# Two on-chip reshapings of an attention, mixer and Fourier kernel moved from TensorE matmuls to small transfers

## The chip, the cores and the metric

The kernel runs on one core of a Trainium2 chip. The metric is the device time of one execution in microseconds; the time before is the median of three executions.

## The reference, cut to what matters

Three blocks follow one another: attention (2 batches, 12 heads, 448 rows, 64 wide), a token and channel mixer, and a block that adds the real part of a two-dimensional Fourier transform, normalises each row and runs a two-layer network of width 3,072.

```python
def _moe2_ref(x, w_ch1, w_ch2):
    X = np.fft.fft(x, axis=1)
    X = np.fft.fft(X, axis=2)
    u = x + np.real(X).astype(np.float32)
    mu = np.mean(u, axis=-1, keepdims=True)
    var = np.mean((u - mu) ** 2, axis=-1, keepdims=True)
    un = (u - mu) / np.sqrt(var + 1e-06)
    ch = np.maximum(un @ w_ch1, 0.0) @ w_ch2
    return (u + ch).astype(np.float32)
```

The change lies in this last block. `x` is 2 x 448 x 768.

## The kernel before

Activations are kept transposed: 768 channels as six tiles of 128 partitions (`resid[ct][b]`), 448 rows of one batch along the free side. Each float32 matmul of the networks is done as three matmuls on split operands (high by high, high by low, low by high), so a 128 x 448 group of the second network costs 18 matmuls going up (`up_chunk`, lines 233 to 235) and 24 going down (`down_tile`, lines 254 to 259). The weights arrive as 64-bit words, are loaded by SyncE's queue into two staging buffers (`fetch`, line 132) and are turned into high and low parts by six steps on ScalarE and VectorE (`convert_steps`).

The middle of the kernel, some 274 to 430 us, is written as one list of words, `ORDER2`. A word names a function and its arguments; each engine, SyncE's queue among them, works off its instructions in the order of the list. The words that matter here:

- `ro b` (`rows_fold`) folds the 448 values of channel 0 of batch b to 225 values in one partition, `r0s[b]`.
- `mr b` (`mean_rows`) turns that row into two columns, of 112 and 113 partitions, by two matmuls with a 1 x 2 block of ones, into a PSUM bank. `rh b` (`rows_high`) casts them on ScalarE, `rl b` (`rows_low`) subtracts on VectorE, and `mx b` (`mixed_mean`) uses them as stationary operands some 17 us later.
- `zh`, `zl`, `oc`, `hi`, `lo` round, split and copy the planes of the Fourier transform and the result; `lo 0.ct` makes `act_l[ct][0]`, which the first groups of the second network (`up2.0`, `up1.0`, ...) need channel tile by channel tile.
- `vm b`, `vr b`, `vi b` give the variance, its root and the inverse deviations `inv[b]`, 112 partitions x 4.
- `dv b` (`deviation`) spreads these over a 128 x 448 PSUM tile by four matmuls against the identity, with each column of `inv[b]` repeated 128 times; `dc b` (`deviation_copy`) copies the tile to `rstd[b]` on ScalarE.
- `dt c.b` (`second_down`) is a group of 24 matmuls, `dm c.b` (`scale`) multiplies its result by `rstd[b]` on VectorE.
- `ld k` loads a weight tile and `cv k.j` is step j of its conversion; `two` closes the buffers of the Fourier stage.

`bank()` hands out the eight PSUM banks in turn. `begin_fft` closes the pools whose buffers the Fourier stage reuses and opens the pool `fft1`.

Of the kernel before, what the change touches and what calls it, by code (L numbers as in the profile page):

```python
# [10 lines left out]
F32 = mybir.dt.float32  # L11
# [8 lines left out]
B, H, S, D = 2, 12, 448, 64  # L20
DM = H * D
TS = 112
NI = S // TS
# [17 lines left out]


ORDER2 = """
ld0 ld1 cv0.0 cv0.1 cv0.2 cv1.0 dn0.3 ad0.3 cv1.1 cv1.2 dn0.4 cv0.3 cv1.3 dn0.0 ad0.0 fs0.0 ad0.4 ro0 dn0.1 fd0.0
dn0.2 fo0.0 ad0.1 ad0.2 fm0.0 fz0 fv0.0 fs0.1 dn0.5 fe0.0 fd0.1 fo0.1 fv0.1 ad0.5 fs0.2 fe0.1 fh0.1 fh0.0 fl0.1 dn1.0
ad1.0 ro1 cv0.4 cv0.5 fl0.0 dn1.3 ad1.3 fm0.1 fs1.0 dn1.4 fd1.0 ld2 ld3 fe0.2 cv1.4 cv1.5 ad1.4 cv2.0 cv2.1 fm0.2 me0
mc0 fm1.0 cv3.0 cv3.1 fz1 fe1.0 fv1.0 fo1.0 dn1.1 fd0.2 ce0.5 ad1.1 fv0.2 cv2.2 fo0.2 ce0.0 dn1.2 ad1.2 fh0.2 dn1.5
ad1.5 fl0.2 fh1.0 fl1.0 fs1.1 fd1.1 fs1.2 fft ch0.0.0 ch0.3.0 ch0.2.0 ch0.2.1 ch0.0.1 ch0.1.0 ch0.1.1 fe1.1 ch0.1.2
zh0.1 fd1.2 fm1.1 fo1.1 fv1.1 ce0.2 zl0.1 ch0.0.2 zh0.0 fh1.1 fl1.1 ce0.4 zl0.0 ch0.2.2 zh0.2 zl0.2 ch0.3.1 ch0.3.2
zh0.3 zl0.3 fm1.2 mr1 mr0 fe1.2 rh1 ch1.2.0 ch1.0.0 ch1.0.1 fo1.2 fv1.2 fh1.2 cv2.3 fl1.2 sq0.0 oc0.0 sq0.1 rh0 oc0.1  # L50
cv2.4 ha0.0 cv3.2 rl1 hs0.0 fa0.0 ch1.0.2 zh1.0 rl0 ch1.3.0 ch1.2.1 ch1.2.2 zh1.2 ce0.1 zl1.0 ha0.1 zl1.2 ch1.1.0
ch1.3.1 ch1.3.2 ch1.1.1 hi0.0 zh1.3 hs0.1 ce0.3 zl1.3 fa0.1 ny0 ch1.1.2 zh1.1 zl1.1 cv2.5 nc0 ba0.0 sq0.2 oc0.2 hi0.1
me1 mc1 sq1.0 oc1.0 ha0.2 ce1.5 hs0.2 fa0.2 sq1.1 oc1.1 ba0.1 lo0.0 lo0.1 ba0.2 hi0.3 hi0.2 ha1.0 ce1.0 hi0.5 lo0.5
lo0.3 lo0.2 hi0.4 lo0.4 ce1.1 hs1.0 cv3.3 fa1.0 ce1.3 ce1.2 ce1.4 ny1 hi1.0 nc1 sq1.2 ba1.0 oc1.2 ha1.1 hs1.1 ha1.2
hs1.2 fa1.1 ba1.1 mx0 fa1.2 ba1.2 mx1 two up2.0 up1.0 cv3.4 cv3.5 up0.0 lo1.0 hi1.4 hi1.3 gh2.0 hi1.1 vs0.1 hi1.2
hi1.5 vs0.0 gh1.0 ma1 ma0 va0.1 vs0.2 va0.2 vs0.3 up3.0 gl1.0 ld4 cv4.0 ld5 cv5.0 cv4.1 cv4.2 cv4.3 ld6 va0.3 cv5.1
cv5.2 vs0.4 va0.4 cv5.3 cv4.4 cv4.5 cv5.4 gh0.0 cv5.5 lo1.3 lo1.1 lo1.2 lo1.4 lo1.5 up3.1 up1.1 up0.1 gl0.0 vs0.5
gl2.0 cv6.0 up2.1 up4.1 up4.0 vs1.0 va0.5 vs1.1 va1.1 gh0.1 gh1.1 cv6.1 cv6.2 gh3.0 gh3.1 vs1.2 va1.2 ld7 cv6.3 cv7.0
cv7.1 vs1.3 va1.3 cv6.4 cv6.5 cv7.2 cv7.3 gl3.0 gh4.1 vs1.4 gh2.1 va1.4 gl3.1 ld8 gh4.0 cv8.0 cv8.1 gl1.1 cv8.2 cv7.4
cv8.3 cv7.5 cv8.4 cv8.5 gl0.1 ld9 cv9.0 cv9.1 cv9.2 cv9.3 up5.0 gh5.0 ld10 cv10.0 up6.1 gh6.1 up7.0 gh7.0 cv10.1 gl5.0  # L60
cv10.2 cv10.3 cv9.4 cv9.5 gl2.1 vs1.5 va1.5 ld11 cv11.0 cv11.1 gl4.1 cv11.2 cv11.3 up6.0 gh6.0 cv10.4 up5.1 vm0 gh5.1
cv10.5 cv11.4 ld12 cv12.0 vr0 up7.1 gh7.1 gl6.0 gl7.0 gl4.0 cv12.1 cv12.2 cv12.3 cv11.5 gl6.1 ld13 cv13.0 gl5.1 cv13.1
cv13.2 cv13.3 vi0 cv12.4 cv12.5 cv13.4 cv13.5 ld14 ld15 vm1 gl7.1 cv14.0 cv14.1 cv14.2 cv14.3 cv15.0 dt0.0 dt0.1
cv15.1 cv15.2 cv15.3 cv14.4 cv15.4 cv14.5 cv15.5 vr1 vi1 ld16 dv0 dc0 cv16.0 ld17 cv17.0 cv16.1 cv16.2 cv16.3 ld18
cv17.1 cv17.2 cv17.3 ld19 dt1.0 dt1.1 dv1 dc1 cv16.4 cv16.5 cv18.0 cv17.4 cv18.1 cv18.2 cv17.5 cv19.0 dm0.0 dt2.1
dm0.1 cv19.1 cv18.3 cv19.2 cv19.3 dt2.0 cv18.4 cv19.4 dt4.0 dp0.5 dp0.0 da0.0 dp1.3 dp1.0 da0.1 dm1.0 dp0.3 da1.0
dm1.1 da1.1 dm2.1 dp1.1 dm2.0 cv18.5 cv19.5 dt4.1 dt3.0 dp0.4 dp0.1 da2.0 dm3.0 da3.0 dt3.1 dt5.0 da2.1 dm3.1 dp1.4
dp0.2 dp1.2 dm4.0 da3.1 dm4.1 da4.0 dm5.0 dp1.5 da5.0 dt5.1 da4.1 dm5.1 da5.1
"""
ENGINES = {getattr(mybir.EngineType, e) for e in ("PE", "DVE", "Activation", "Pool", "SP")}  # L70

# [31 lines left out]
def fused_kernel(ctx: ExitStack, tc: tile.TileContext, qk, v, w1, w2, wa, wb, wc, wd, fa, fb, out):  # L103
    nc = tc.nc
    mm = nc.tensor.matmul
    vec, act, pool = nc.vector, nc.scalar, nc.gpsimd
# [161 lines left out]
    with ExitStack() as actx:  # L268
# [6 lines left out]
            out=mask[:, S - TS :], in_=mask[:, S - TS :], pattern=[[-1, TS]], compare_op=ALU.is_ge, fill=MASKED,  # L275
# [313 lines left out]
    pb, uv, ab, r0s = {}, {}, {}, {}  # L589
# [59 lines left out]
    f1 = [None]  # L649
# [44 lines left out]
    rows_of = {}  # L694

    def mean_rows(b):
        rp = bank()
        pb["r", b] = [(TS + i, rp[: TS + i, 2 * i : 2 * i + 2]) for i in range(2)]
        for i, (rows, part) in enumerate(pb["r", b]):
            mm(part, lhsT=r0s[b][:, i * TS : i * TS + rows], rhs=ones[:, :2], start=True, stop=True)  # L700

    def rows_high(b):
        rows_of[b] = [
# [98 lines left out]
    inv, rstd, g2, pools = {}, [], {}, {}  # L802
# [64 lines left out]

    def mean_back(b, ct):
        pool.tensor_tensor(out=resid[ct][b], in0=resid[ct][b], in1=mu[b], op=ALU.add)
# [2 lines left out]
        dn=down, ad=down_add, ro=rows_fold, fs=fold_sum, fd=fold_difference, fe=fold_ends, fv=fold_even,  # L872
        fo=fold_odd, fh=fold_high, fl=fold_low, fm=fold_mean, fz=fold_zero, fft=begin_fft, ch=channel, zh=z_high, zl=z_low,
        me=mean, mc=mean_copy, ce=center, mr=mean_rows, rh=rows_high, rl=rows_low, mx=mixed_mean, ma=mixed_add,
        sq=sequence, ny=nyquist, nc=nyquist_copy, fa=forward_add, oc=odd_copy, ha=half_add, hs=half_subtract, ba=backward_add, hi=high,
        lo=low, ld=load_second, cv=convert_second, two=begin_second, up=lambda m, b: second_up(m, b, 0),
        gh=lambda m, b: second_up(m, b, 1), gl=lambda m, b: second_up(m, b, 2), vs=square, va=square_add, vm=variance,
        vr=root, vi=inverse, dt=second_down, dm=scale, da=scaled, dv=deviation, dc=deviation_copy, dp=mean_back,
    )
    with tc.manual_schedule(engines=ENGINES):  # L880
        for word in ORDER2.split():
            name = word.rstrip("0123456789.")
# [98 lines left out]
```

## Time and profile before

| what | value |
|---|---|
| time before, median of 3 (range) | 674.91 us (674.77 to 675.99) |
| the profiled execution | 674.54 us |
| span of its profile | 672.8 us |
| TensorE busy | 668.2 us, 99% of the span, 3,702 matmul records |
| VectorE busy | 533.9 us, 79% |
| ScalarE busy | 282.7 us, 42% |
| GpSimd busy | 111.3 us, 17% |
| TensorE's granted clock, mean | 0.999 of full speed |
| DMA | 73.35 MB, mean 109 GB/s |

The span runs from the first to the last instruction of the profiled execution; 1.74 us of its own time lie outside the span. One float32 matmul of the program can appear as two records. Matmuls overlap in the records, so what one costs is read from the distance between starts, not from its duration.

### The profile page before, as it was taken

How to read it: one execution, taken by the hardware profiler on the slowest of the kernel's cores; microseconds unless marked ns; L12 is line 12 of the kernel's file. 1: busy time of each engine (PE TensorE's matmuls, PEld its weight loads, DVE VectorE, ACT ScalarE, POOL GpSimd, SP SyncE). 2: the span in 40 equal slices, each digit the busy share in tenths (PEclk: the TensorE clock that was granted, in tenths of full speed). 3: DMA queues.
4: the chain of work that ended last, by engine and by line, in shares of the span. 5: the costliest groups of instructions: out<-in, count | busy, mean ns of one | idle time of the engine just before them, and what ended most of it. 6: DMA issues, size and time to landing. Idle time of an engine off the chain costs nothing.

```text
span 672.8 us, 9833 instructions
## 1 busy us (share of the span) xinstructions
PE 668.2 (99%) x3702; PEld 607.1 (90%) x3702; DVE 533.9 (79%) x1016; ACT 282.7 (42%) x601; POOL 111.3 (17%) x86
## 2 busy tenths in 40 slices
PE   9999999999999999999999999999999999999997
PEld 6777778999999999999999999999999999999997
DVE  7988876678988955899899859989878898656851
ACT  7989785433343333235465432224432334332200
POOL 0042343310000000400510007271002320000000
PEclk9999999999999999999999999999999999999999
DMA  8532221194344331200224332423332543222311
GB/s 222 189 137 70 102 75 64 39 280 142 116 166 141 126 109 48 95 0 1 95 95 145 105 127 94 141 94 120 114 123 72 181 140 123 84 92 77 118 41 55
DMA packets 20863, 73.35 MB, mean 109 GB/s; under 512 B 2366, under 2 KB 7230, under 8 KB 20448
## 3 DMA queue, kind: packets, MB, share of 16 engines
q1 hardware_dynamic: 20240, 69.48, 30.5%
q0 software_dynamic: 576, 3.25, 1.7%
q8 instruction: 29, 0.48, 0.3%
q14 instruction: 18, 0.15, 0.1%
HBM read 69.96 MB, written 2.75 MB: 108 GB/s over the span
## 4 chain that ended last, share of the span: by engine, by line
PE 99%; DMA 0%; DVE 0%; SPq 0%; issue 0%
PE psum L234 13%; PE psum L258 13%; PE psum L233 13%; PE psum L254 13%; PE psum L259 13%; PE psum L235 13%; PE psum L314 4%; PE psum L367 4%; PE psum L349 4%; PE psum L436 3%; PE psum L470 2%; PE psum L672 2%; PE psum L741 1%; PE psum L387 1%; PE psum L456 1%; DMA k<-in_qk 0%
## 5 line engine op out<-in xcount | busy, mean ns | idle before, releaser
L254 PE MATMUL psum<-gh,wh 128*128 128x448 f32 x432 | 157.2, 364 | 0.0
L233 PE MATMUL psum<-acth,wh 128*128 128x448 f32 x432 | 156.9, 363 | 0.0
L234 PE MATMUL psum<-acth,wl 128*128 128x448 f32 x432 | 156.4, 362 | 0.0
L258 PE MATMUL psum<-gh,wl 128*128 128x448 f32 x432 | 156.4, 362 | 0.0
L259 PE MATMUL psum<-gl,wh 128*128 128x448 f32 x432 | 156.0, 361 | 0.0
L235 PE MATMUL psum<-actl,wh 128*128 128x448 f32 x432 | 155.9, 361 | 0.0
L141 ACT ACTIVATE m<-w 128x512 f32<-128x512 f32 (+2 forms) x92 | 70.9, 771 | 125.4 <-DVE wl L161 83.4
L159 ACT CAST wh<-m 128x512 fp32r<-128x512 f32 (+1 forms) x90 | 63.3, 704 | 95.2 <-PE psum L259 53.6
L254 PEld LDWEIGHTS psum<-gh,wh 128*128 128x128 f32 x432 | 81.1, 188 | 5.8 <-issue 0.2
L233 PEld LDWEIGHTS psum<-acth,wh 128*128 128x128 f32 x432 | 81.1, 188 | 5.7
L235 PEld LDWEIGHTS psum<-actl,wh 128*128 128x128 f32 x432 | 80.9, 187 | 5.8
L259 PEld LDWEIGHTS psum<-gl,wh 128*128 128x128 f32 x432 | 80.9, 187 | 5.8
L258 PEld LDWEIGHTS psum<-gh,wl 128*128 128x128 f32 x432 | 81.0, 187 | 5.0 <-issue 0.2
L234 PEld LDWEIGHTS psum<-acth,wl 128*128 128x128 f32 x432 | 81.0, 188 | 4.6
L148 DVE SCALAR_TENSOR_TENSOR m<-w,m 128x512 uint32<-128x512 uint32 (+2 forms) x92 | 80.2, 872 | 2.3
L161 DVE TENSOR_TENSOR wl<-m,wh 128x512 fp32r<-128x512 f32 (+1 forms) x84 | 69.4, 829 | 14.7 <-ACT wh L159 14.3
L152 DVE SCALAR_TENSOR_TENSOR m<-w,m 128x512 uint32<-128x512 uint32 (+2 forms) x92 | 79.2, 861 | 2.0
L143 DVE TENSOR_SCALAR m<-m 128x512 f32<-128x512 f32 (+2 forms) x92 | 50.8, 552 | 34.4 <-ACT m L141 34.2
L241 DVE SCALAR_TENSOR_TENSOR gl<-psum,gh 128x448 fp32r<-128x448 f32 x72 | 43.6, 618 | 27.2 <-ACT gh L239 27.2
L239 ACT ACTIVATE gh<-psum 128x448 fp32r<-128x448 f32 x72 | 37.8, 540 | 63.1 <-PE psum L235 62.7
L337 ACT ACTIVATE p<-p,small 112x224 f32<-112x224 f32 (+3 forms) x96 | 49.6, 520 | 3.9 <-DVE small L327 3.8
L144 DVE TENSOR_SCALAR m<-m 128x512 uint32<-128x512 uint32 (+2 forms) x92 | 48.9, 532 | 2.4
(146 smaller groups left out, 741.1 us busy)
## 6 DMA issues: line engine op xcount, KB each, us to landing
w<-in_wc SPq DMA_DIRECT2D x24, 768.0 KB, 4.2
w<-in_wd SPq DMA_DIRECT2D x36, 512.0 KB, 3.2
w<-in_wa SPq DMA_DIRECT2D x12, 768.0 KB, 4.3
w<-in_wb SPq DMA_DIRECT2D x18, 512.0 KB, 3.2
v<-in_v SPq DMA_DIRECT2D x12, 224.0 KB, 2.8
out<-t SPq DMA_DIRECT2D x12, 224.0 KB, 1.9
q<-in_qk SPq DMA_DIRECT2D x11, 224.0 KB, 3.4
k<-in_qk SPq DMA_DIRECT2D x11, 224.0 KB, 3.5
```

Of the source, the lines that this page charges most:

```text
L141: act.activation(out=m, in_=hi.bitcast(F32), func=AF.Abs)
L143: vec.tensor_scalar(out=m, in0=m, scalar1=F64_MIN, scalar2=F64_MAX, op0=ALU.max, op1=ALU.min)
L148: vec.scalar_tensor_tensor(out=mu, in0=lo, scalar=29, in1=mu, op0=ALU.logical_shift_right, op1=ALU.bitwise_or)
L152: vec.scalar_tensor_tensor(out=mu, in0=hi, scalar=0xC0000000, in1=mu, op0=ALU.bitwise_and, op1=ALU.bitwise_or)
L159: act.copy(wh, m)
L161: low_engine[0].tensor_tensor(out=wl, in0=m, in1=f(wh), op=ALU.subtract)
L233: mm(pb[:, :S], lhsT=lh, rhs=act_h[ct][b], start=ct == 0, stop=False)
L234: mm(pb[:, :S], lhsT=ll, rhs=act_h[ct][b], start=False, stop=False)
L235: tail[0] = mm(pb[:, :S], lhsT=lh, rhs=act_l[ct][b], start=False, stop=ct == NCT - 1).ins
L254: mm(pb[:, :S], lhsT=lh, rhs=gh, start=j + k == 0 and seeded is None, stop=False, skip_group_check=seeded is not None,)
L258: mm(pb[:, :S], lhsT=ll, rhs=gh, start=False, stop=False, skip_group_check=seeded is not None)
L259: tail[0] = mm(pb[:, :S], lhsT=lh, rhs=gl, start=False, stop=j == last and k == nk - 1, skip_group_check=seeded is not None,).ins
```

## The change

`mean_rows` no longer runs matmuls. It takes a small SBUF tile from the pool `fft1` and fills its two columns by two transfers on SyncE's queue, from 112 and from 113 values of the one-partition row. `rows_high` and `rows_low` read the SBUF tile, each column repeated twice, instead of PSUM.

`deviation` writes `inv[b]` into a row of 448 floats in HBM, one value for each partition and column, and `deviation_copy` reads that row back into all 128 partitions of `rstd[b]`; both are transfers on SyncE's queue. The words move in `ORDER2`: `dv0 dc0` from behind `ld16` to behind `ld15` and ahead of `vm1`; `dv1 dc1` from behind `dt1.1` to behind `ld17`. The place of `mr1 mr0` is unchanged. The rest of `ORDER2` keeps its order (the diff also wraps its lines anew).

```diff
-cv13.2 cv13.3 vi0 cv12.4 cv12.5 cv13.4 cv13.5 ld14 ld15 vm1 gl7.1 cv14.0 cv14.1 cv14.2 cv14.3 cv15.0 dt0.0 dt0.1
-cv15.1 cv15.2 cv15.3 cv14.4 cv15.4 cv14.5 cv15.5 vr1 vi1 ld16 dv0 dc0 cv16.0 ld17 cv17.0 cv16.1 cv16.2 cv16.3 ld18
-cv17.1 cv17.2 cv17.3 ld19 dt1.0 dt1.1 dv1 dc1 cv16.4 cv16.5 cv18.0 cv17.4 cv18.1 cv18.2 cv17.5 cv19.0 dm0.0 dt2.1
...
+ld13 cv13.0 gl5.1 cv13.1 cv13.2 cv13.3 vi0 cv12.4 cv12.5 cv13.4 cv13.5 ld14 ld15 dv0 dc0 vm1 gl7.1 cv14.0 cv14.1
+cv14.2 cv14.3 cv15.0 dt0.0 dt0.1 cv15.1 cv15.2 cv15.3 cv14.4 cv15.4 cv14.5 cv15.5 vr1 vi1 ld16 cv16.0 ld17 dv1
+dc1 cv17.0 cv16.1 cv16.2 cv16.3 ld18 cv17.1 cv17.2 cv17.3 ld19 dt1.0 dt1.1 cv16.4 cv16.5 cv18.0 cv17.4 cv18.1
...
+    scratch = ctx.enter_context(tc.tile_pool(name="scratch", bufs=1, space=bass.MemoryType.DRAM))
...
     def mean_rows(b):
-        rp = bank()
-        pb["r", b] = [(TS + i, rp[: TS + i, 2 * i : 2 * i + 2]) for i in range(2)]
-        for i, (rows, part) in enumerate(pb["r", b]):
-            mm(part, lhsT=r0s[b][:, i * TS : i * TS + rows], rhs=ones[:, :2], start=True, stop=True)
+        rp = f1[0].tile([113, 16], F32, name=f"rows{b}")
+        pb["r", b] = [(TS + i, rp[: TS + i, i : i + 1].to_broadcast([TS + i, 2])) for i in range(2)]
+        for i in range(2):
+            nc.sync.dma_start(out=rp[: TS + i, i : i + 1], in_=r0s[b][:, i * TS : (i + 1) * TS + i])
...
     def deviation(b):
-        pb["w", b] = bank()[:, :S]
-        for i in range(NI):
-            mm(
-                pb["w", b][:, i * TS : (i + 1) * TS], lhsT=inv[b][:, i : i + 1].to_broadcast([TS, 128]),
-                rhs=ident[:TS, :TS], start=True, stop=True,
-            )
+        pb["w", b] = scratch.tile([1, S], F32, name=f"dev{b}")
+        nc.sync.dma_start(out=pb["w", b][0].rearrange("(i p) -> p i", p=TS), in_=inv[b])
 
     def deviation_copy(b):
-        act.copy(rstd[b], pb["w", b])
+        nc.sync.dma_start(out=rstd[b], in_=pb["w", b].to_broadcast([128, S]))
```

## Rows read from the trace of the kernel before

**Rows 1.** The page, part 4: the chain that ended last, by engine.

```profile
PE 99%; DMA 0%; DVE 0%; SPq 0%; issue 0%
```

**Rows 2.** Timeline, TensorE, 300.9 to 302.6: start us, us, line, what, count.

```profile
300.78 0.33 PE L672 MATMUL psum<-fal,acth 128*111 128x384 f32 x1
300.95 0.33 PE L672 MATMUL psum<-fah,actl 128*111 128x384 f32 x1
301.21 0.94 PE L700 MATMUL psum<-ones,r 1*112 1x2 f32 x8
302.09 0.43 PE L672 MATMUL psum<-fah,acth 128*113 128x386 f32 x1
302.36 0.34 PE L672 MATMUL psum<-fal,acth 128*113 128x386 f32 x1
```

**Rows 3.** Timeline, TensorE, around the two groups of deviation().

```profile
388.52 0.37 PE L259 MATMUL psum<-gl,wh 128*128 128x448 f32 x1
388.73 1.04 PE L860 MATMUL psum<-ident,r 112*128 112x112 f32 x8
...
389.83 0.36 PE L258 MATMUL psum<-gh,wl 128*128 128x448 f32 x1
...
399.03 0.37 PE L259 MATMUL psum<-gl,wh 128*128 128x448 f32 x1
...
400.33 0.36 PE L258 MATMUL psum<-gh,wl 128*128 128x448 f32 x1
```

**Rows 4.** Waits of TensorE, whole span: us in total, times, longest.

```profile
PE psum L195 <- PEq L968: 0.8, 1, 0.8
```

**Rows 5.** Timeline, VectorE, four places (in brackets: idle before, releaser).

```profile
308.15 0.22 DVE L713 TENSOR_TENSOR repl<-psum,reph 112x2 fp32r<-112x2 f32 x2
...
312.53 0.56 DVE L680 TENSOR_TENSOR zl<-psum,zh 112x384 fp32r<-112x384 f32 x1 [0.56 <-ACT zh L676]
...
320.44 0.62 DVE L784 TENSOR_TENSOR actl<-resid,acth 128x448 fp32r<-128x448 f32 x1
...
329.23 0.94 DVE L161 TENSOR_TENSOR wl<-m,wh 128x768 fp32r<-128x768 f32 x1
```

**Rows 6.** Timeline, TensorE, two places of the first `up` groups.

```profile
321.51 0.36 PE L235 MATMUL psum<-actl,wh 128*128 128x448 f32 x1
...
330.70 0.36 PE L233 MATMUL psum<-acth,wh 128*128 128x448 f32 x1
330.91 0.36 PE L234 MATMUL psum<-acth,wl 128*128 128x448 f32 x1
```

**Rows 7.** Timeline, ScalarE, 301 to 307: the casts of rows_high.

```profile
301.80 0.22 ACT L708 CAST reph<-psum 112x2 fp32r<-112x2 f32 x2
...
305.55 0.23 ACT L708 CAST reph<-psum 112x2 fp32r<-112x2 f32 x2
```

**Rows 8.** Source line 601, the folded row: ns min/median/max, first and last start.

```profile
L601 DVE TENSOR_TENSOR r<-resid x2: 371/372/373, 274.9 to 283.2; 1x223 f32<-1x223 f32 x2
```

**Rows 9.** Timeline, SyncE's DMA issues, three places.

```profile
248.76 23.87 SPq L132 DMA_DIRECT2D w<-in_wc  x4
...
382.07 0.33 SPq L132 DMA_DIRECT2D w<-in_wd  x1
...
393.84 0.33 SPq L132 DMA_DIRECT2D w<-in_wd  x1
```

**Rows 10.** Source line 841, last step of the inverse deviations.

```profile
L841 DVE TENSOR_TENSOR r<-r,nt x2: 161/162/164, 382.8 to 391.4; 112x4 f32<-112x4 f32 x2
```

**Rows 11.** Source line 851, the first reader of rstd in scale().

```profile
L851 DVE TENSOR_TENSOR t<-psum,rstd x12: 606/616/625, 405.0 to 455.3; 128x448 f32<-128x448 f32 x12
```

**Rows 12.** DMA issues of the span: count, KB each, median us to landing.

```profile
out<-t SPq DMA_DIRECT2D x12, 224.0 KB, 1.9
...
k<-in_qk SPq DMA_DIRECT2D x11, 224.0 KB, 3.5
```

**Rows 13.** DMA queue, 0 to 4 us: packets, MB, share of 16 engines.

```profile
q1 hardware_dynamic: 593, 0.49, 52.4%
```

More of the change, by code (lines that the diff above doesn't have):

```diff
@@ L43 @@
 ORDER2 = """
[L44 to L62, printed above, removed]
-cv13.2 cv13.3 vi0 cv12.4 cv12.5 cv13.4 cv13.5 ld14 ld15 vm1 gl7.1 cv14.0 cv14.1 cv14.2 cv14.3 cv15.0 dt0.0 dt0.1
@@ L64 @@
-cv15.1 cv15.2 cv15.3 cv14.4 cv15.4 cv14.5 cv15.5 vr1 vi1 ld16 dv0 dc0 cv16.0 ld17 cv17.0 cv16.1 cv16.2 cv16.3 ld18
-cv17.1 cv17.2 cv17.3 ld19 dt1.0 dt1.1 dv1 dc1 cv16.4 cv16.5 cv18.0 cv17.4 cv18.1 cv18.2 cv17.5 cv19.0 dm0.0 dt2.1
-dm0.1 cv19.1 cv18.3 cv19.2 cv19.3 dt2.0 cv18.4 cv19.4 dt4.0 dp0.5 dp0.0 da0.0 dp1.3 dp1.0 da0.1 dm1.0 dp0.3 da1.0
-dm1.1 da1.1 dm2.1 dp1.1 dm2.0 cv18.5 cv19.5 dt4.1 dt3.0 dp0.4 dp0.1 da2.0 dm3.0 da3.0 dt3.1 dt5.0 da2.1 dm3.1 dp1.4
-dp0.2 dp1.2 dm4.0 da3.1 dm4.1 da4.0 dm5.0 dp1.5 da5.0 dt5.1 da4.1 dm5.1 da5.1
+ld0 ld1 cv0.0 cv0.1 cv0.2 cv1.0 dn0.3 ad0.3 cv1.1 cv1.2 dn0.4 cv0.3 cv1.3 dn0.0 ad0.0 fs0.0 ad0.4 ro0 dn0.1
@@ new lines @@
+fd0.0 dn0.2 fo0.0 ad0.1 ad0.2 fm0.0 fz0 fv0.0 fs0.1 dn0.5 fe0.0 fd0.1 fo0.1 fv0.1 ad0.5 fs0.2 fe0.1 fh0.1 fh0.0
+fl0.1 dn1.0 ad1.0 ro1 cv0.4 cv0.5 fl0.0 dn1.3 ad1.3 fm0.1 fs1.0 dn1.4 fd1.0 ld2 ld3 fe0.2 cv1.4 cv1.5 ad1.4
+cv2.0 cv2.1 fm0.2 me0 mc0 fm1.0 cv3.0 cv3.1 fz1 fe1.0 fv1.0 fo1.0 dn1.1 fd0.2 ce0.5 ad1.1 fv0.2 cv2.2 fo0.2
+ce0.0 dn1.2 ad1.2 fh0.2 dn1.5 ad1.5 fl0.2 fh1.0 fl1.0 fs1.1 fd1.1 fs1.2 fft ch0.0.0 ch0.3.0 ch0.2.0 ch0.2.1
+ch0.0.1 ch0.1.0 ch0.1.1 fe1.1 ch0.1.2 zh0.1 fd1.2 fm1.1 fo1.1 fv1.1 ce0.2 zl0.1 ch0.0.2 zh0.0 fh1.1 fl1.1 ce0.4
@@ new lines @@
+zl0.0 ch0.2.2 zh0.2 zl0.2 ch0.3.1 ch0.3.2 zh0.3 zl0.3 fm1.2 mr1 mr0 fe1.2 rh1 ch1.2.0 ch1.0.0 ch1.0.1 fo1.2
+fv1.2 fh1.2 cv2.3 fl1.2 sq0.0 oc0.0 sq0.1 rh0 oc0.1 cv2.4 ha0.0 cv3.2 rl1 hs0.0 fa0.0 ch1.0.2 zh1.0 rl0 ch1.3.0
+ch1.2.1 ch1.2.2 zh1.2 ce0.1 zl1.0 ha0.1 zl1.2 ch1.1.0 ch1.3.1 ch1.3.2 ch1.1.1 hi0.0 zh1.3 hs0.1 ce0.3 zl1.3
+fa0.1 ny0 ch1.1.2 zh1.1 zl1.1 cv2.5 nc0 ba0.0 sq0.2 oc0.2 hi0.1 me1 mc1 sq1.0 oc1.0 ha0.2 ce1.5 hs0.2 fa0.2
+sq1.1 oc1.1 ba0.1 lo0.0 lo0.1 ba0.2 hi0.3 hi0.2 ha1.0 ce1.0 hi0.5 lo0.5 lo0.3 lo0.2 hi0.4 lo0.4 ce1.1 hs1.0
@@ new lines @@
+cv3.3 fa1.0 ce1.3 ce1.2 ce1.4 ny1 hi1.0 nc1 sq1.2 ba1.0 oc1.2 ha1.1 hs1.1 ha1.2 hs1.2 fa1.1 ba1.1 mx0 fa1.2
+ba1.2 mx1 two up2.0 up1.0 cv3.4 cv3.5 up0.0 lo1.0 hi1.4 hi1.3 gh2.0 hi1.1 vs0.1 hi1.2 hi1.5 vs0.0 gh1.0 ma1 ma0
+va0.1 vs0.2 va0.2 vs0.3 up3.0 gl1.0 ld4 cv4.0 ld5 cv5.0 cv4.1 cv4.2 cv4.3 ld6 va0.3 cv5.1 cv5.2 vs0.4 va0.4
+cv5.3 cv4.4 cv4.5 cv5.4 gh0.0 cv5.5 lo1.3 lo1.1 lo1.2 lo1.4 lo1.5 up3.1 up1.1 up0.1 gl0.0 vs0.5 gl2.0 cv6.0
+up2.1 up4.1 up4.0 vs1.0 va0.5 vs1.1 va1.1 gh0.1 gh1.1 cv6.1 cv6.2 gh3.0 gh3.1 vs1.2 va1.2 ld7 cv6.3 cv7.0 cv7.1
@@ new lines @@
+vs1.3 va1.3 cv6.4 cv6.5 cv7.2 cv7.3 gl3.0 gh4.1 vs1.4 gh2.1 va1.4 gl3.1 ld8 gh4.0 cv8.0 cv8.1 gl1.1 cv8.2 cv7.4
+cv8.3 cv7.5 cv8.4 cv8.5 gl0.1 ld9 cv9.0 cv9.1 cv9.2 cv9.3 up5.0 gh5.0 ld10 cv10.0 up6.1 gh6.1 up7.0 gh7.0 cv10.1
+gl5.0 cv10.2 cv10.3 cv9.4 cv9.5 gl2.1 vs1.5 va1.5 ld11 cv11.0 cv11.1 gl4.1 cv11.2 cv11.3 up6.0 gh6.0 cv10.4
+up5.1 vm0 gh5.1 cv10.5 cv11.4 ld12 cv12.0 vr0 up7.1 gh7.1 gl6.0 gl7.0 gl4.0 cv12.1 cv12.2 cv12.3 cv11.5 gl6.1
+ld13 cv13.0 gl5.1 cv13.1 cv13.2 cv13.3 vi0 cv12.4 cv12.5 cv13.4 cv13.5 ld14 ld15 dv0 dc0 vm1 gl7.1 cv14.0 cv14.1
@@ new lines @@
+cv14.2 cv14.3 cv15.0 dt0.0 dt0.1 cv15.1 cv15.2 cv15.3 cv14.4 cv15.4 cv14.5 cv15.5 vr1 vi1 ld16 cv16.0 ld17 dv1
+dc1 cv17.0 cv16.1 cv16.2 cv16.3 ld18 cv17.1 cv17.2 cv17.3 ld19 dt1.0 dt1.1 cv16.4 cv16.5 cv18.0 cv17.4 cv18.1
+cv18.2 cv17.5 cv19.0 dm0.0 dt2.1 dm0.1 cv19.1 cv18.3 cv19.2 cv19.3 dt2.0 cv18.4 cv19.4 dt4.0 dp0.5 dp0.0 da0.0
+dp1.3 dp1.0 da0.1 dm1.0 dp0.3 da1.0 dm1.1 da1.1 dm2.1 dp1.1 dm2.0 cv18.5 cv19.5 dt4.1 dt3.0 dp0.4 dp0.1 da2.0
+dm3.0 da3.0 dt3.1 dt5.0 da2.1 dm3.1 dp1.4 dp0.2 dp1.2 dm4.0 da3.1 dm4.1 da4.0 dm5.0 dp1.5 da5.0 dt5.1 da4.1
@@ L69 @@
+dm5.1 da5.1
 """
```

## The prediction

> **What bounds the kernel now.** I read the page first, then TensorE's timeline around the three places that the change empties, TensorE's waits, the timelines of the engines that feed it there, and the DMA views. The page's chain of work that ended last is TensorE for 99% of the span [rows 1]: there is no second limit behind which a saving on TensorE could hide. The waits say the same. In the whole span TensorE has one listed wait, of 0.8 us, at the very start [rows 4]. So in the stretch of the change (300 to 405 us) every matmul starts as soon as the one ahead lets it, and the question is in two halves: how much time the removed matmuls take there, and whether the other engines can follow a TensorE that arrives earlier, and are not themselves delayed by the transfers.
>
> **What leaves TensorE.** I read a cost from the starts of the matmuls on either side, since durations overlap.
>
> Rows of channel 0. The last two transform matmuls ahead start at 300.78 and 300.95, a pitch of 0.17 to 0.18 us. Two more would start by 301.30; the second one behind the eight records of line 700 starts at 302.36 [rows 2]. The two `mr` words cost 302.36 - 301.30 = 1.06 us.
>
> Inverse deviations. The pitch of a 448-column matmul is 0.20 us (330.70 to 330.91 [rows 6]). From 388.52 the second matmul on would start at 388.92 and starts at 389.83: 0.91 us. For batch 1, from 399.03, it would start at 399.43 and starts at 400.33: 0.90 us [rows 3].
>
> Sum: 1.06 + 0.91 + 0.90 = 2.87 us. The third matmul behind each group is at the old pitch again, so nothing more is in it.
>
> The eight records with two columns start within 0.94 us, some 0.12 us each [rows 2]. The Trainium skill ("TensorE: Matmul & The Clock Gate", section "Back-to-back issue gap") puts the spacing of matmuls of 1 to 64 columns at about 60 cycles, some 25 ns. By it the eight would be worth about 0.2 us, the gain 2.0 us and the time 672.9; the row disagrees, and the row decides.
>
> ScalarE loses two copies, and with them the place where it stands behind `dv1`. VectorE's conversions behind that may run earlier. No wait of TensorE hangs on them [rows 4], so I give this nothing. PSUM: four bank allocations go. The bank of every remaining allocation is taken again by the eighth behind it, and removing allocations only moves that one later; banks get looser, not tighter.
>
> **Can the feeders keep up with the earlier TensorE?** Removing 1.06 us at 301 asks everything behind to be 1.06 us earlier. The tightest place that I found is the first group `up2.0`. Its third low-part matmul starts at 321.51 [rows 6] and reads `act_l[2][0]`, which VectorE makes from 320.44 to 321.06 [rows 5]: 0.45 us of room. VectorE has one idle time in the stretch before, 0.56 us at 312, ended by ScalarE's `zh` [rows 5], which itself waits for a transform matmul that now comes 1.06 us earlier. That idle time should go, and VectorE be 0.56 us earlier. New need: 321.51 - 1.06 = 320.45. New ready: 321.06 - 0.56 = 320.50. So I charge 0.05 us of new waiting; if VectorE does not move, 0.61. The next tightest is the low part of weight 3: ready at 329.23 + 0.94 = 330.17 [rows 5], needed at 330.91 [rows 6], 0.74 of room; with both shifts 0.24 remains.
>
> **What the transfers add.** No matmul waits for a transfer directly; ScalarE, VectorE and SyncE do.
>
> Row transfers. They stand on SyncE's queue behind `ld3`, issued by 272.6 (248.76 + 23.87, [rows 9]), and ahead of `ld4`, which waits for `two` behind the last use of these rows; so nothing queues behind them that they could delay. The second folded row is ready at 283.2 + 0.37 = 283.6 [rows 8]. They also need their SBUF tile's old contents to be read; at the latest that is when batch 1's last `dn` ends and the transform begins: the 36 matmuls of `ch0`, at 0.175 us, end about 301.1 [rows 2], so begin about 295. Their price is not in the trace. Lower bound nothing, if they are done before ScalarE asks at 301.80 [rows 7]. For the upper I use the shortest transfers there are: in the first 4 us 593 packets of 0.8 KB on average took 52.4% of 16 engines [rows 13], 0.524 x 16 x 4 / 593 = 0.057 us each. If all 113 values of a column go one after the other on one engine, that is 6.4 us, plus some 2 us (1.9 us is the quickest landing, [rows 12]). From 283.6, two batches are in by 300; from 295, at 304 and 311. The nearer case is the early issue with shorter packets, so I take nothing.
>
> Deviations, batch 0. `inv[0]` is ready at 382.96 [rows 10], SyncE is free from 382.4 (`ld15`, [rows 9]). Writing 448 single values: 28 packets for each of 16 engines, 1.6 us at 0.057, plus 1.9 to 3.5 us of landing [rows 12], so in HBM by 386.5 to 388. The read-back is 224 KB, like `k` or `out`: 1.9 to 3.5 us more [rows 12]. `rstd[0]` stands by 392, and its first reader starts at 405.0 [rows 11]: at least 13 us to spare.
>
> Deviations, batch 1. Ready at 391.5 [rows 10], in `rstd[1]` by 391.5 + 5.1 + 0.4 + 3.5 = 400.5 at worst, still ahead of 405. Behind the waiting `dc1` on SyncE's queue stands `ld18`, issued at 393.84 before [rows 9]; it slips by up to 3 us. Its weight is for `dt5`, six groups of 24 matmuls behind 399.2 [rows 3], 399.2 + 6 x 4.8 = 428, so this costs nothing.
>
> The Trainium skill ("DMA: Bandwidth & Descriptors", section "Anatomy of one DMA") gives each transfer about 2 us of fixed time; two hops would then take some 4 to 5 us, an estimate inside the bounds above.
>
> **Sum.** 674.54 - 2.87 + 0.05 = 671.72 for the profiled execution. That execution is 0.37 us below the median shown, 674.91, so in the median's terms 672.1 us.
>
> **The rivals.**
>
> 1. *The row saving is handed back at `up2.0`.* VectorE is busy without a break from there to 331 but for the one idle time, so if that remains, 0.6 of the 1.06 us returns as a wait of TensorE on line 784; if ScalarE is also held a little at `rows_high`, all of it. For it: 0.45 us of room is small. Against: the idle time is released through TensorE. Time: 672.6 to 673.2.
>
> 2. *The row transfers come late and the kernel gets slower.* ScalarE and VectorE stand in order at `rows_high` and `rows_low`; VectorE reaches the second `rows_low` at 308.15 [rows 5], behind a cast that took 0.2 us. A second pair landing at time L later than 307.9 stops VectorE, and past the 0.45 us of room every microsecond stops TensorE. Against the 1.81 us that the deviations save, the kernel breaks even at L = 307.9 + 0.45 + 1.81 = 310.2. With late issue (295) and one engine for 113 values at 0.057 us each, L is 311 and the time about 675.7. For it: both halves of this are possible. Against: four-byte packets should be shorter than 0.8 KB ones, and the queue is free from 283.6 on. The Trainium skill ("DMA: Bandwidth & Descriptors", section "Why a DMA increments its semaphore by 16 and not by 1") says that a transfer is spread over the largest number of engines up to 16 that divides the outer sizes. 113 is prime, so by this rule the longer column does go through one engine. No row here shows it.
>
> 3. *The write of the deviations is slow and holds SyncE's queue.* If all 448 values went through one engine, 448 x 0.057 = 25.5 us, `dc0` would hold the queue until about 411 and `ld16`, issued between 382 and 394 before [rows 9], would follow it. Its weight is for `dt4`, due at 399.2 + 2 x 4.8 = 409, and with 3.5 us of landing [rows 12] and six conversion steps of under 0.94 us each [rows 5] would come 9 us late or so: 681. It decides once the two hops take over about 15 us. Against: 112 partitions divide well, and 15 us is four times the slowest ordinary landing.
>
> 4. *The change frees nothing.* TensorE's weight loads or its sequencer would fill the gap, and the time stays at 674.9. Against: each removed group shows as a step in the starts.
>
> **How the numbers follow.** The forecast has 0.74, its own range being 671.5 to 672.6; rival 1 has 0.13; rival 2, 0.05; rival 3, 0.03; rival 4, 0.05. A measurement of this kernel can tell about 0.2%, 1.35 us, from no change. The forecast and rival 1 lie beyond that (faster 0.87), rival 4 inside (0.05), rivals 2 and 3 I count as slower, 0.08 together. The range takes the forecast and rival 1, 0.87 of the chance, with a few tenths at either end, since the median before could itself stand 1 us higher (range to 675.99): 671.2 to 673.4.
>
> **What would show it.** Right: no records of lines 700 and 860 on TensorE; starts at the old pitch across the three places; the same `up2.0` and `dt2.1` matmuls about 1.0 and 2.8 us earlier; no new wait of TensorE above a tenth or so. Wrong: a wait of TensorE on line 784 at about 320 (rival 1), a long idle of ScalarE ahead of line 708 ended by a DMA (rival 2), `ld16` or `ld18` issued much later or an idle of VectorE ahead of line 851 ended by a DMA (rival 3).

## The result

The changed kernel takes 682.17 us in the median (681.16 to 683.03, five executions) against 674.91 us: a ratio of 1.0104, with a 95% interval of 1.0093 to 1.0115. It is 1% slower where the prediction had it 0.4% faster. One execution each of *dev_split* (831.22 us) and *re16* (952.79 us) below and two of the kernel before (1731.51 and 3255.49 us) were far slower than the others of their kernel and are in none of the medians.

The profiled execution of the changed kernel took 683.03 us. The line numbers of its profile are three higher than before. Its chain of the work that ended last is no longer TensorE alone (before: [rows 1]):

```profile
PE 77%; DVE 13%; DMA 4%; issue 3%; ACT 2%; POOL 1%; SPq 0%; ACTq 0%; DVEq 0%; POOLq 0%
```

and where TensorE waited once before [rows 4], its waits now are (us in total, times, longest):

```profile
PE psum L257 <- ACT wh L162: 3.1, 1, 3.1
PE psum L236 <- DVE t L854: 1.8, 1, 1.8
PE psum L261 <- DVE wl L164: 1.3, 1, 1.3
PE psum L262 <- DVE gl L244: 1.1, 1, 1.1
PE psum L198 <- PEq L967: 0.8, 1, 0.8
```

Four new waits, 7.3 us together: first for the high and the low part of a weight (lines 162 and 164), then, at the first group of the next network stage, for a PSUM bank that `scale()` had not yet emptied (line 854), then for an operand (line 244). What the weights wait for is on SyncE's queue, whose issues are these (start, duration, line; before: [rows 9]):

```profile
296.26 2.76 SPq L703 DMA_DIRECT2D rows<-r  x4
...
383.61 0.34 SPq L862 DMA_DIRECT2D dev<-r  x1
391.45 0.34 SPq L865 DMA_DIRECT2D rstd<-dev  x1
391.89 0.85 SPq L135 DMA_DIRECT2D w<-in_wd  x2
392.79 1.59 SPq L862 DMA_DIRECT2D dev<-r  x1
405.57 0.33 SPq L865 DMA_DIRECT2D rstd<-dev  x1
406.00 0.85 SPq L135 DMA_DIRECT2D w<-in_wd  x2
```

Each `rstd<-dev` stands for the moment at which the write ahead of it was complete: 391.45 and 405.57, that is 7.8 and 12.7 us behind their issues. `ld16` and `ld17` follow at 391.9, the last two weights at 406.0; before, they were all out by 396.5. The source view of the two lines gives the same landing times, of the write (first) and of the read-back:

```profile
DMA to landing us min/median/max: 7.8/10.2/12.7
...
DMA to landing us min/median/max: 6.0/6.0/6.0
```

The DMA view of the stretch from 386.3 to 391.4 shows what the write does in that time:

```profile
DMA packets 0, 0.00 MB, mean 0 GB/s; under 512 B 0, under 2 KB 0, under 8 KB 0
```

Nothing starts. The packets of the first write were all begun by 386, soon after `ld15` had gone through; then some 5.6 us pass in which the transfer is not complete, and SyncE stands at `dc0`. ScalarE, which converts the weights, waits for them meanwhile (timeline; idle time and releaser in brackets):

```profile
398.67 0.66 ACT L144 ACTIVATE m<-w 128x512 f32<-128x512 f32 x1 [7.89 <-DMA w<-in_wd]
...
412.98 0.66 ACT L144 ACTIVATE m<-w 128x512 f32<-128x512 f32 x1 [10.56 <-DMA w<-in_wd]
```

and TensorE runs out of work at 410.7 (timeline):

```profile
414.20 0.47 PE L257 MATMUL psum<-gh,wh 128*128 128x448 f32 x1 [3.14 <-ACT wh L162]
415.95 0.74 PE L261 MATMUL psum<-gh,wl 128*128 128x448 f32 x1 [1.28 <-DVE wl L164]
```

After that idle time the clock is lower for a while (stretch; length; then busy us and count of TensorE, its weight loads, VectorE, ScalarE and GpSimd; the mean granted clock as a share of 2.4 GHz; share and rate of the DMA):

```profile
410.00:415.00 5.00, 1.53 (x7) 0.83 (x5) 1.25 (x3) 1.17 (x2) 0.00 (x0) 1.00 0.61 221
415.00:425.00 10.00, 9.05 (x38) 8.38 (x39) 9.93 (x11) 1.91 (x3) 7.13 (x6) 0.83 0.23 79
```

A mean of 0.83 over 10 us, in which the engine was at 1.2 GHz for a part, is some 1.7 us of full speed lost.

The balance, from TensorE's starts. From the first transform matmul to `up2.0` the changed kernel takes 24.43 us, before 25.10: the row transfers gain 0.67. From `dt0.0` to the last matmul it takes 297.62 us, before 289.70: the deviations lose 7.92. That is 1.81 of matmuls removed, 7.3 of waits and 1.7 of clock added, and 0.7 of slower starts behind each wait. -0.67 + 7.92 = 7.25 us; the medians differ by 7.26. The two profiled executions differ by 8.49 us, because the transform also begins 1.24 us later in the changed one (296.03 instead of 294.79); that part comes from the first 15 us of the execution, long before the change.

### The profile page after: what moved, and what is told of

Read it like the earlier page. It is cut to its first block, busy times and chain, and to the rows that moved or that the text cites. A ratio compares the mean times of both kernels' runs of the same rounds, so it can differ in the third digit from the quotient of the medians.

```text
span 681.3 us, 9803 instructions
## 1 busy us (share of the span) xinstructions
PE 669.2 (98%) x3678; PEld 605.9 (89%) x3678; DVE 534.0 (78%) x1016; ACT 281.7 (41%) x599; POOL 112.0 (16%) x86
## 4 chain that ended last, share of the span: by engine, by line
PE 77%; DVE 13%; DMA 4%; issue 3%; ACT 2%; POOL 1%; SPq 0%; ACTq 0%; DVEq 0%; POOLq 0%
PE psum L238 10%; PE psum L236 10%; PE psum L237 10%; PE psum L262 9%; PE psum L257 9%; PE psum L261 9%; PE psum L317 4%; PE psum L370 4%; PE psum L352 4%; DVE m L151 3%; PE psum L439 2%; PE psum L473 2%; DVE wl L164 2%; DMA dev<-r 2%; DVE m L146 2%
```

## The experiments

In all of them the same two distances can be taken from the trace, which are free of what varies from one execution to the next: the transform begins anywhere between 294.8 and 296.5 us in these profiles. "Rows" is the distance from the first transform matmul to `up2.0`, "deviations" that from `dt0.0` to the last matmul; the write's landing is the median of two, both from one profiled execution. Each ratio below is taken against executions of the kernel before from the same session, whose medians were 674.94, 674.58 and 675.70 us in the three sessions.

| run | rows, us | deviations, us | write lands, us | median, us |
|---|---|---|---|---|
| before | 25.10 | 289.70 | no write | 674.91 |
| changed | 24.43 | 297.62 | 10.2 | 682.17 |
| rows_only | 24.43 | 289.70 | no write | 674.99 |
| dev_only | 25.10 | 297.57 | 8.9 | 682.38 |
| dev_split | 24.43 | 291.88 | 9.7 | 677.30 |
| dev_pool | 24.42 | 292.32 | 8.7 | 677.75 |
| write_only | 25.10 | 290.33 | 10.2 | 676.32 |
| hbm_16b | 24.46 | 287.89 | 2.3 | 672.30 |
| hbm_sparse | 24.46 | 287.89 | 2.6 | 672.27 |
| hbm_step16 | 24.43 | 287.89 | 3.4 | 672.28 (one) |
| dense_filled | 24.43 | 298.42 | 10.6 | 682.80 (one) |
| sbuf_hop | 24.43 | 287.89 | 2.3 (to SBUF) | 673.21 |
| re16 | 24.42 | 287.89 | 2.6 | 673.25 |
| re16_mm | 25.10 | 287.89 | 2.5 | 673.03 |

### Which half of the change

*rows_only*: `deviation`, `deviation_copy` and `ORDER2` as before, `mean_rows` as changed.

> The kernel before with the row transfers alone; the inverse deviations go by matmuls and ScalarE copies as before. Theory H (the whole loss comes from the slow write of the deviations, which holds SyncE's queue for 7.8 and 12.7 us and makes the weight loads behind it late): TensorE saves the 1.06 us of line 700 and hands back at most 0.6, so 673.9 to 674.5. Rival R (the row transfers cost something too, through ScalarE and VectorE at 303 to 309 us): 676 or more.

Measured: 674.99 us, ratio 0.9999 (0.9991 to 1.0008). The big loss is not here, as theory H said. The time itself shows no gain; the trace shows 0.67 us in the stage. What takes part of the 1.06 us back is one place, in VectorE's and TensorE's timelines of this run:

```profile
306.44 0.63 DVE L637 TENSOR_TENSOR actl<-ab,acth 128x448 fp32r<-128x448 f32 x1
...
306.66 0.34 PE L672 MATMUL psum<-fal,acth 128*112 128x386 f32 x1
307.12 0.43 PE L672 MATMUL psum<-fah,actl 128*112 128x386 f32 x1
307.39 0.33 PE L672 MATMUL psum<-fah,acth 128*111 128x384 f32 x1
```

The matmul at 307.12 needs the low part that VectorE ends at 307.07 (`fl1.2`). It comes 0.46 us behind the one ahead rather than 0.17 to 0.18, and the next 0.27: 0.38 us in all. 1.06 - 0.38 = 0.68.

*dev_only*: the changed kernel with this put back.

```diff
     def mean_rows(b):
-        rp = f1[0].tile([113, 16], F32, name=f"rows{b}")
...
+        rp = bank()
+        pb["r", b] = [(TS + i, rp[: TS + i, 2 * i : 2 * i + 2]) for i in range(2)]
+        for i, (rows, part) in enumerate(pb["r", b]):
+            mm(part, lhsT=r0s[b][:, i * TS : i * TS + rows], rhs=ones[:, :2], start=True, stop=True)
```

> The changed kernel with the matmuls of mean_rows put back; only the deviations go by transfers. Theory H: the loss stays whole, about 683 (682.17 plus the 1 us of the matmuls). Rival R: at least half of the 7 us goes with the row transfers, 679 or less.

Measured: 682.38 us, ratio 1.0106 (1.0093 to 1.0119). The whole loss is in the deviations.

### The wait on SyncE's queue, or the transfers themselves

*dev_split*: the same transfers, with the words parted.

```diff
-ld15 dv0 dc0 ... ld17 dv1 dc1 ... ld19
+ld15 dv0 ... ld17 dc0 dv1 ... ld19 dc1
```

> The changed kernel, same transfers, but dv and dc are parted on SyncE's queue so that the wait for the write stands where no load is due: dv0 behind ld15, dc0 and dv1 behind ld17, dc1 behind ld19. Theory H: the loads are issued as in the kernel before (ld16 to ld19 by about 397), TensorE does not wait, and the whole 2.2 to 2.9 us of matmuls is gained: 671.8 to 673. Rival L (it is the late rstd itself, through scale() and the PSUM banks, not the queue): the write and the read-back take as long as they do, rstd of batch 1 comes at about 404 or later, and the time stays at 679 or more.

Measured: 677.30 us, ratio 1.0037 (1.0024 to 1.0050), between the two theories. SyncE now waits 4.4 us for the writes where it waited 18.6, and the loss falls by 4.9 us. But the writes still land 8.5 and 10.9 us behind their issues, the last read-back starts at 402.49, and TensorE waits for a bank at the first group of the next stage:

```profile
PE psum L210 <- DVE t L828: 2.1, 1, 2.1
```

(line 210 is the first matmul of `up_chunk` here, line 828 `scale()`). Rival L put such a wait down to the late `rstd`. The chain of work that leads to this wait shows something else (start, duration, what; cut to the pieces that matter):

```profile
386.56 7.62 DMA w<-in_wd
...
397.36 8.28 DMA w<-in_wd
...
408.63 1.07 DVE t L828 x2
...
444.56 1.08 DVE t L828 x2
...
445.77 0.44 PE psum L210
```

It goes through two weight loads that took 7.62 and 8.28 us instead of 3.2 to 3.3, the conversions of these weights, the `scale()` that stands behind the conversions in VectorE's order, and later conversions and another load, up to the bank. No transfer of `rstd` is in it: the last one, for batch 1, landed at 408.61, 0.5 us before its first use. So the late weights make `scale()` late, not the late `rstd`.

*dev_pool*: the same transfers on another queue.

```diff
-        nc.sync.dma_start(out=pb["w", b][0].rearrange("(i p) -> p i", p=TS), in_=inv[b])
+        pool.dma_start(out=pb["w", b][0].rearrange("(i p) -> p i", p=TS), in_=inv[b])
...
-        nc.sync.dma_start(out=rstd[b], in_=pb["w", b].to_broadcast([128, S]))
+        pool.dma_start(out=rstd[b], in_=pb["w", b].to_broadcast([128, S]))
```

> The changed kernel with the four transfers of the deviations issued from GpSimd's queue, which is idle until the first scaled() at about 405; SyncE's queue is free of their waits. Theory H: loads on time, 672 to 673.5 (the transfers themselves may take longer from there, with some 5 us to spare). Rival L: 679 or more.

Measured: 677.75 us, ratio 1.0042 (1.0026 to 1.0057). Here SyncE waits for no write at all, and the time is still 5.6 us above the 672.1 predicted, again between the two theories. GpSimd's timeline has the two writes, each followed by a wait (7.0 and 10.1 us):

```profile
383.46 0.76 POOL L862 DMA_DIRECT2D dev<-r  x1 [47.20 <-issue]
391.24 0.57 POOL L865 DMA_DIRECT2D rstd<-dev  x1 [7.02 <-DMA dev<-r]
391.81 0.73 POOL L862 DMA_DIRECT2D dev<-r  x1
402.65 0.55 POOL L865 DMA_DIRECT2D rstd<-dev  x1 [10.11 <-DMA dev<-r]
```

And ScalarE waits for weights although no write holds their queue. `ld16` is issued on time, at 386.81, and lands 7.3 us later; the next pair, which needs the staging buffers, goes out at 397.27, and its first load lands 8.9 us later; the wait ahead of that pair's first conversion is 8.34 us long and ends at 406.27. So theory H, as I had put it, was half the cause. A slow write holds the queue, but it also does something to the loads beside it. Theory M (a write of small neighbouring pieces is itself slow and slows the loads meanwhile) came from here.

### What the write does to other transfers

*write_only*: the kernel before, matmuls kept, with a write that nobody reads.

```diff
+    def spare_write(b):
+        row = scratch.tile([1, S], F32, name=f"dev{b}")
+        nc.sync.dma_start(out=row[0].rearrange("(i p) -> p i", p=TS), in_=inv[b])
...
-ld15 ... ld17
+ld15 dw0 ... ld17 dw1
```

> The kernel before, matmuls and ScalarE copies kept, with the two writes of the deviations to HBM added behind ld15 and ld17 and read by nobody. It shows what the write does to the other transfers by itself, as nobody waits for it. Theory M: the loads issued while a write drains (ld16, ld17, then ld18) land in 6 to 8 us instead of 3.3, and the time is 675 to 676, since the conversions have a few us to spare. Rival H (only the wait on SyncE's queue did harm, the loads themselves were not slowed): ld16 to ld19 land in 3.3 us as before and the time is unchanged, 674.9.

Measured: 676.32 us, ratio 1.0019 (1.0010 to 1.0028). The five weight loads of 380 to 405 us land like this (source lines of the tile `w`; the one at 3.2 was issued ahead of the write), against 3.2 to 3.3 us in the kernel before:

```profile
DMA to landing us min/median/max: 3.2/7.6/8.6
```

The DMA view from 387 to 394.9 shows it (the rate in 40 slices of 0.2 us); `ld16` is issued at 387.00, `ld17` at 389.25:

```profile
GB/s 0 0 0 0 41 228 145 249 0 0 0 0 0 0 0 0 83 145 62 21 21 62 21 41 41 0 62 62 41 373 290 62 83 249 373 415 415 436 373 333
...
w<-in_wd SPq DMA_DIRECT2D x2, 512.0 KB, 7.1
dev<-r SPq DMA_DIRECT2D x1, 1.8 KB, 10.7
```

The load begins, stops, and crawls until the write of 383.02 is through, 9.7 us after its issue. Nobody waits for that write; the loads suffer all the same. This is as theory M has it.

`rstd` is made by matmuls here, and is ready at 400.8. Even so VectorE reaches the first `scale()` at 408.91, where it was 404.96 in the kernel before, straight from the conversion of a late weight (line 137):

```profile
408.31 0.68 DVE L137 TENSOR_TENSOR wl<-m,wh 128x512 fp32r<-128x512 f32 x1
408.91 1.15 DVE L827 TENSOR_TENSOR t<-psum,rstd 128x448 f32<-128x448 f32 x2
```

That is as late as in *dev_split* (408.55) and *dev_pool* (409.09): the slow loads alone delay `scale()` by some 4 us. The profile is of the fastest of ten executions (674.99 us) and has only 0.63 us of loss in "deviations"; where the others lose more was not seen.

### Why the write is slow

*hbm_16b*: the four deviations of a partition go as one piece.

```diff
-        nc.sync.dma_start(out=pb["w", b][0].rearrange("(i p) -> p i", p=TS), in_=inv[b])
+        nc.sync.dma_start(out=pb["w", b][0].rearrange("(p i) -> p i", i=NI), in_=inv[b])
```

> The changed kernel, order of words and all, but the 448 deviations of a batch are written to HBM as 112 pieces of 16 bytes (each partition's four together) instead of 448 pieces of 4 bytes. The read-back is the same, so rstd holds the deviations in another order of rows. Theory M (small pieces written to one short stretch of HBM drain one after another, 5.6 us for 448 here, some 12 ns each, and hold up the other loads meanwhile): 112 pieces drain in about 1.4 us, the write lands within some 4 to 6 us of its issue (most of it behind the load in front), ld16 and ld17 land in 3 to 5 us, and the time falls from 682 to 673 to 677. Rival N (any write to HBM takes that long to be acknowledged, whatever its pieces): the write stays at 8 and 12 us and the time at 681 or more.

Measured: 672.30 us, ratio 0.9964 (0.9952 to 0.9976). TensorE has no wait in the stretch. The write lands in

```profile
DMA to landing us min/median/max: 1.9/2.3/2.7
```

so it is not the way to HBM as such: rival N falls. Both numbers are better than theory M's (4 to 6 us, 673 to 677): a price for each piece, taken from the slow write, does not hold here. *hbm_16b*, *hbm_sparse* and *hbm_step16* put other values into `rstd` than the deviations; they are here for their times alone.

*hbm_sparse*: 448 pieces of 4 bytes as in the changed kernel, but 64 bytes apart, in a row of HBM that is 16 times as long and is filled at `mr`.

```diff
-        nc.sync.dma_start(out=pb["w", b][0].rearrange("(i p) -> p i", p=TS), in_=inv[b])
+        nc.sync.dma_start(out=pb["w", b][0].rearrange("(i p e) -> p i e", p=TS, e=16)[:, :, 0], in_=inv[b])
```

> The changed kernel with the 448 four-byte pieces written 64 bytes apart, over 28 KB of HBM that is filled earlier; the read-back takes the first 448 floats, so rstd holds other values than the deviations. If theory M is right because neighbouring pieces fall into the same short lines and wait for each other, the write lands several us sooner than 7.8 and 12.7 us and the loads behind it are quicker. If each small piece costs its time wherever it goes, the write and the time (about 682) stay as in the changed kernel.

Measured: 672.27 us, ratio 0.9970 (0.9955 to 0.9985). As many pieces, as small, and

```profile
DMA to landing us min/median/max: 2.2/2.6/2.9
```

So neither the number nor the size of the pieces alone makes the write slow. What does is that 448 pieces of 4 bytes lie next to each other in HBM, 4 bytes from start to start.

*dense_filled*: the row of the changed kernel, filled at `mr` too, the pieces 4 bytes apart.

> The changed kernel with its 1.8 KB rows in HBM filled once, earlier, by another transfer, as the run with pieces 64 bytes apart has it; the pieces stay next to each other. If the distance of the pieces is what matters, the writes land at 8 us or more and the time is 680 to 683. If the earlier filling is what helped there, the writes land in 2 to 4 us and the time is 672 to 673.

Measured, one execution: 682.80 us. The earlier filling changes nothing; the DMA view has

```profile
dev<-r SPq DMA_DIRECT2D x2, 1.8 KB, 10.6
```

*hbm_step16*: as *hbm_sparse*, with `e=4`, so 16 bytes apart.

> The changed kernel with its 448 four-byte pieces written 16 bytes apart, over 7 KB of HBM filled earlier; rstd holds other values than the deviations. Between the two ends (4 bytes apart: 7.8 and 12.7 us; 64 bytes apart: 2.6 us). If pieces wait for each other where they share a stretch of 64 bytes, four to a stretch should land in 3 to 5 us, and the time is 672 to 675; if sharing at all is what costs, it is near the changed kernel's.

Measured, one execution: 672.28 us, and

```profile
DMA to landing us min/median/max: 3.0/3.4/3.7
```

The distances stand in order: the same 448 pieces of 4 bytes land in 10.2 us at 4 bytes apart, 3.4 at 16, 2.6 at 64. The 112 pieces of 16 bytes, whose starts are 16 bytes apart too, land in 2.3.

### Versions that keep the computation

*sbuf_hop*: gather into one SBUF partition, one piece to HBM, read back.

```diff
     def deviation(b):
-        pb["w", b] = scratch.tile([1, S], F32, name=f"dev{b}")
-        nc.sync.dma_start(out=pb["w", b][0].rearrange("(i p) -> p i", p=TS), in_=inv[b])
+        for i in range(NI):
+            nc.sync.dma_start(out=pb["dev"][b : b + 1, i * TS : (i + 1) * TS], in_=inv[b][:, i : i + 1])
+
+    def deviation_row(b):
+        pb["w", b] = scratch.tile([1, S], F32, name=f"dev{b}")
+        nc.sync.dma_start(out=pb["w", b], in_=pb["dev"][b : b + 1])
...
-ld15 dv0 dc0 ... ld16 ... ld17 dv1 dc1 ... ld18 ... ld19
+ld15 dv0 ... ld16 dx0 ... ld17 dc0 dv1 ... ld18 dx1 ... ld19 dc1
```

> The changed kernel with the deviations first gathered into one partition of SBUF by four transfers of 112 four-byte pieces, then written to HBM as one piece of 1.8 KB, then read back; the three steps are parted on SyncE's queue (gather behind ld15 and ld17, write behind ld16 and ld18, read-back behind ld17 and ld19), so that little is waited for there. Theory M: gather and write land in some 2 us each, the loads are not slowed, rstd of batch 1 stands by about 402, and the time is 672 to 674. Rival N: the write to HBM takes 5 us or more even in one piece, rstd comes at 407 or later, and the time is 676 or more.

Measured: 673.21 us, ratio 0.9971 (0.9961 to 0.9980), faster than either kernel. The gather consists of 448 four-byte pieces side by side, in SBUF, and lands in

```profile
DMA to landing us min/median/max: 1.9/2.3/2.8
```

so pieces side by side are not slow in SBUF. (The gather is four transfers of 112 pieces each; no run wrote so few pieces of 4 bytes side by side to HBM.)

*re16*: pieces of 16 bytes as in *hbm_16b*, put in order by GpSimd.

```diff
+    def deviation_order(b):
+        pool.tensor_copy(
+            out=rstd[b].rearrange("q (i p) -> q i p", i=NI), in_=pb["wr", b].rearrange("q (p i) -> q i p", i=NI)
+        )
...
-ld15 dv0 dc0 ... ld17 dv1 dc1 ... ld19
+ld15 dv0 ... ld17 dc0 dy0 dv1 ... ld19 dc1 dy1
```

> The changed kernel with the deviations written as 112 pieces of 16 bytes, read back in that order into a tile of their own, and put in order by one strided copy for each batch on GpSimd, which is idle there; the steps are parted on SyncE's queue (dv0 behind ld15, dc0 and dv1 behind ld17, dc1 behind ld19). Theory M: write and read-back are quick, rstd of batch 1 stands by about 403, the time is 672 to 673.2. Rival (the detour over GpSimd makes rstd late again, or its copy slows VectorE): 674 or more.

Measured: 673.25 us, ratio 0.9963 (0.9949 to 0.9978). The copies take 1.20 and 0.98 us on GpSimd, the second `scale()` waits 0.69 us for one, and TensorE for neither.

*re16_mm*: the same with the matmuls of `mean_rows`.

> The same with the matmuls of mean_rows put back, so that it differs from the run before by the row transfers alone. Their worth by the trace of the kernel with the row transfers alone is 0.68 us (1.06 less a new wait of 0.38 at the transform): 0.4 to 1.0 us slower than its twin. If the row transfers are worth nothing: within 0.3 us of it.

Measured: 673.03 us, ratio 0.9963 (0.9949 to 0.9977): 0.2 us below its twin, so the expectation of 0.4 to 1.0 us above it failed. In the traces the stage itself is 24.42 us with the transfers and 25.10 without, as in every other run of either kind. But the transform begins at 296.45 in the one profile and at 295.14 in the other, and such a difference hides 0.7 us. It does not come from the row transfers: TensorE's starts from 15 us on to the transform agree within 0.02 us in the two profiles, and so do those of *before* and *rows_only*; the difference arises in the first 15 us. From the first transform matmul to the last matmul of all it is 371.45 us with the row transfers and 372.13 without. So in the traces the 0.68 us do reach the last matmul; the times do not confirm it, as what varies in the first 15 us and behind the last matmul (3.9 to 4.7 us) is larger.

## Why the prediction was wrong

**The matmuls removed.** Right. The deviations' 1.81 us are gained to the hundredth where nothing waits (289.70 - 287.89 in six runs), and the matmuls of TensorE next behind the rows' place come 1.06 us earlier. By the Trainium skill's spacing ("TensorE: Matmul & The Clock Gate", section "Back-to-back issue gap") the gain of the rows would have been 0.2 us; the trace has 0.67 even after the new wait. The page calls that spacing the gap of an isolated matmul and says that it counts too little at small widths, having no room for weight loads; each of the eight records here had its own weight load, so the 0.2 us were no fair reading of it.

**The tightest place.** Off in its size and place. I charged 0.05 us at `up2.0`; 0.38 us arose earlier, at the transform, for `fl1.2`. It could have been read before: VectorE's low part of `fl1.2` against the third matmul that follows it had 0.83 us of room, less than the 1.06 us asked for. I had stopped at the first tight place that I found.

**The row transfers.** Right that they are hidden, but not for the reason given. I had taken the early issue, at 283.6; they were issued at 296.26, just behind the first transform matmul (296.03), which is the late case of rival 2. What saved them is the price:

```profile
rows<-r SPq DMA_DIRECT2D x2, 0.4 KB, 2.0
```

They land in 2.0 us (two of the four have a landing on record) where my upper end had 8.4, and the casts in `rows_high`, at 303.0, start without a wait.

**The price of the write.** This is the step that failed. "Writing 448 single values: 28 packets for each of 16 engines, 1.6 us at 0.057, plus 1.9 to 3.5 us of landing, so in HBM by 386.5 to 388." The packets did start as quickly as that; the transfer was complete at 391.45, and for batch 1 at 405.57. The price was to be 3.5 to 5.1 us and was 7.8 and 12.7. The rows that I took as the nearest ones were loads into SBUF and stores of whole rows; none of them wrote small pieces side by side to HBM, and the upper end taken from them was not an upper end. A page bears on it: the Trainium skill ("DMA: Bandwidth & Descriptors", section "Specifications") has transfers below 512 B done by a read-modify-write. Pieces that share a short stretch of memory might then have to wait for one another, and the runs at 4, 16 and 64 bytes fit that; but that this is the mechanism was not shown. What was shown is that the distance decides, and why it does stays open.

**What stands behind the wait.** Underrated. For batch 0, I had `dc0` done at about the time `ld16` was due and so saw only `ld18` slip, by up to 3 us. In fact `ld16` slipped by 4.9 us and `ld18` by 12.2. Rival 3 described this outcome, a held queue and late weights, and had 0.03; its reason, one engine for all pieces, is not the one found, since pieces farther apart are quick with the same shape of transfer. Its 681 us came near by other numbers: it had one write of 25.5 us, and the runs have two waits of 18.6 us together.

**What the sum left out.** Two things that no term covered. The loads beside a slow write are slowed (3.2 to 7.6 us, with nobody waiting for the write). And late weights matter even where no matmul waits for them: their conversions stand ahead of `scale()` in VectorE's order, and in *dev_split* the chain from there leads on to the next stage, where TensorE waits 2.1 us for the last bank. I had checked `rstd` against its first reader, and that check held: in no run with the slow write did `scale()` wait for it, and VectorE's idle time ahead of `scale()`, one of the signs that the prediction named for rival 3, did not come. I had not asked what else stands ahead of that reader. With the queue freed the kernel takes 677.75 (*dev_pool*), so the hold is worth some 4.4 us; from there to 672.27 (*hbm_sparse*) the slow loads and what follows from them are worth some 5.5. These are differences of medians; in the profiles the "deviations" column falls by 5.3 and by 4.4.

With the pieces kept apart or made four times as long, the change gains about what was forecast: 672.27 and 672.30 us, against 672.1 predicted. By the distances the gain is 1.81 + 0.64 = 2.45 us, against 2.82 forecast. These two kernels put other values into `rstd`; the ones that keep the computation take 673.0 to 673.3.

## What to carry to other kernels

A small transfer's cost is not in its bytes: before a matmul is replaced by a write to HBM, ask how its pieces lie there, and make neighbours one piece or keep them apart (or gather in SBUF first). Price a transfer that the trace does not contain by a measurement, or leave its upper end open; where a DMA wait is put on a queue, list the loads behind it and beside it; and follow what each late load delays, engine by engine in its order of work, to where the bounding engine meets it next. On an engine with no idle time, check every operand within the distance that you want to gain, not the first tight one.

## What the runs showed of the hardware

- 448 writes of 4 bytes side by side into 1.8 KB of HBM complete 7.2 to 13.0 us after issue (six runs), in the changed kernel 5.6 us after the last of the first write's packets began; 16 bytes apart, 3.0 to 3.7 us; 64 bytes apart, 2.2 to 2.9; 112 writes of 16 bytes side by side, 1.9 to 3.1 (three runs); 448 pieces of 4 bytes side by side in SBUF, in four transfers, 1.9 to 2.8.
- While such a write is incomplete, 512 KB loads on the same queue land in up to 8.6 us instead of 3.2 (*write_only*), and they are slowed as well, to 7.3 and 8.9 us, when the write comes from GpSimd's queue (*dev_pool*).
- Reading one 1.8 KB row of HBM into 128 partitions took 4.6 to 6.8 us beside the slow writes and 3.4 to 4.5 us without them.
